# Half-chunk score loads, other places for fills, sums and weight passes, and another order of the first FFN matmuls in a fused scan and feed-forward kernel

## The chip, the cores and the metric

One core of one Trainium2 chip runs the whole kernel. The metric is the device time of one execution in microseconds (us), as a median over runs. The engines are named as in the profile: PE is TensorE (matmuls, with PEld for its weight loads), DVE is VectorE, ACT is ScalarE, POOL is GpSimd, and SP is SyncE, which here only issues DMAs. Each engine works through its own list in order; semaphores tie the lists together.

## The reference

Two parts follow each other. The first is a chunked linear-attention scan over 4 batches, 8 heads and 768 tokens, with head size 32 and state size 16; the second is a feed-forward network (FFN) on the 3072 tokens by 256 channels that come out of it. Cut to what matters:

```python
log_a = np.log(np.clip(a, 1e-06, 1.0))
for c in range(nc):                                   # chunks of tokens
    cum = np.cumsum(la, axis=-1)
    L = np.exp(cum[..., :, None] - cum[..., None, :]) * causal
    CB = np.einsum('bhin,bhjn->bhij', Cc, Bc)
    y_intra = np.einsum('bhij,bhjd->bhid', CB * L, xc)
    y_inter = np.einsum('bhin,bhnd->bhid', Cc, state) * np.exp(cum)[..., None]
    y[:, :, sl] = y_intra + y_inter
    state = decay_full * state + np.sum(Bx * decay_from_j, axis=2)

h = x @ w_in                                          # 256 -> 2048
g = np.maximum(0.01 * h, h)
out = g @ w_out                                       # 2048 -> 256
```

All of it is in float32.

## The kernel before, in words

The scan is cut into **units**: one chunk of 96 tokens of one batch, with its 8 heads. There are 8 chunks of 4 batches, so 32 units, and unit `u` is batch `u % 4` of chunk `u // 4`. A unit needs four things in turn. `decay_direct` (units 0 and 1) or `decay_pe` (units 2 to 15) makes the exponent of the decay mask on PE, and `decay_of` takes its exponential on ACT into the tile `lt`. `scores` multiplies B and C on PE, in two halves, and DVE multiplies each half onto `lt` (L314). `unit_products` multiplies the result with x and makes the next state (L326, L335). `unit_halves` copies the output, rounded to a high part `xh`, on ACT, puts the state into the next chunk's tile by way of POOL (L360), and subtracts on DVE to get the low part `xl` (L365). Units 16 to 31 take another way to their decay mask and are done in pairs between FFN steps (`pair_block`).

**The lead** is everything up to the first FFN step: the constants, the sums of the log decays, and units 0 to 14. Its loop stands at L619. In round `u` it issues the scores of unit `u + 1`, the decay mask of unit `u + 2` and the products of unit `u`. `fill_later` and `fill_less` write constant rows into the operands `dl` and `dr` of `decay_pe`, of which there are two sets, for 2 and for 4 units (`ROWS`); other rows of them come by DMA from the sums, which `split_sums` cuts into three bf16 parts and writes to DRAM (L605) and `decay_rows_of` reads back (L242, L245). Set 0 is used by units 2 and 3, set 1 by units 4 to 7. `keep_warm` issues a dummy matmul that nothing reads (L110). `score_tile` hands out one of two PSUM buffers of two banks each; a unit's scores use both.

**The FFN** works in 96 steps, each one tile of 512 tokens (`t`) with one block of 128 hidden columns (`f`); the first 21 steps go through `f` = 0 to 6 for three token tiles in turn, so steps 0, 1, 2 share `f` = 0. A step has two halves that stand apart: `ffn_in` (6 matmuls at L512 into a PSUM tile `hp`), and, three steps later (`LAG`), `ffn_out` (6 matmuls at L540). Between them ACT writes the activation's high part `gh` (L519) and the activation itself in place (L522), and DVE subtracts the two to get the low part `gl` (L525). Every float32 product is made of three: high times high, low weight times high, high weight times low. `hp` comes from `ps_h`, which has two buffers; steps 2 and 3 take a score tile instead.

**The weights** of a block `f` arrive as 64-bit floats in `raw` (512 KB, `fetch_w`) and are decoded by ACT and DVE: `decode_abs` on ACT, then five DVE *passes* in the order hold (L416), shift (L422), sign (L429), low (L436), rest (L449), with ACT's `decode_high` (L442) before rest. `rest` writes the low half `wl`. The passes stand in one queue; `LEAD_PASSES` says in which rounds of the lead one pass each is taken from it, and `PASSES` how many are taken after each FFN step. At step 0 two more are taken ahead of unit 15.

**The order** of all this is the order in which the code is written: the scheduler is switched off (`manual_schedule`), so each engine gets its instructions, and SP its DMAs, in the order of the calls.

## Time and profile before

| | us |
|---|---|
| Timed runs | 325.27, 325.07, 323.19 (median 325.07) |
| The profiled execution: own time / span in the profile | 323.83 / 322.1 |
| PE busy / its share of the span | 315.7 / 98% |
| DVE, ACT, POOL busy | 163.7, 167.4, 75.5 |
| First FFN matmul starts at | 36.72 |
| Its first `ffn_out` matmul starts at | 42.26 |

Times in the profile count from the start of the span. A row of the timeline reads: start, duration, engine, line, operation, output and inputs, shapes, count, and in brackets the idle time ahead of it and what ended it. Matmuls are pipelined, so a row of several matmuls is longer than the distance to the next, and distances of starts are the safer measure. A row of the chain of waits reads: start, length, what the time went to.

### The profile page before, as it was taken

To read this page: it belongs to the slowest core of one execution; us is meant where nothing else is said; L and a number is where in the kernel's file an instruction comes from. 1 tells how busy PE (TensorE), PEld (TensorE's weight loads), DVE (VectorE), ACT (ScalarE), POOL (GpSimd) and SP (SyncE) were. 2 spreads that over 40 slices of the span, in tenths; PEclk is the share of its full clock that TensorE was granted. 3 is DMA by queue.
4 is the path that set the end of the run, shared out by engine and by line. 5 is a ranking of instruction groups with operands and counts; after the bars stand their busy time and mean duration, and the time that the engine had idled before them with its cause. 6 is when DMAs were issued, how large, how long until landed. Compare 5 with 4: busy or idle time off the path is not lost.

```text
span 322.1 us, 6238 instructions
## 1 busy us (share of the span) xinstructions
PE 315.7 (98%) x2425; PEld 250.4 (78%) x2425; DVE 163.7 (51%) x312; ACT 167.4 (52%) x335; POOL 75.5 (23%) x162
## 2 busy tenths in 40 slices
PE   8999999999999999999999999999999999999995
PEld 4566688888887877788778788888878788888884
DVE  6878899888889325425352352524352322322221
ACT  5567686666576555454634636363633444444431
POOL 4377610000000163264330434344210000000000
PEclk9999999999999999999999999999999999999999
DMA  5687244323540830408120062202010000100001
GB/s 177 191 256 242 67 132 130 130 85 113 196 155 14 250 79 7 146 2 240 68 87 0 36 207 67 87 2 86 2 65 0 2 0 2 65 1 0 2 1 65
DMA packets 11497, 27.86 MB, mean 87 GB/s; under 512 B 2283, under 2 KB 2763, under 8 KB 11467
## 3 DMA queue, kind: packets, MB, share of 16 engines
q1 hardware_dynamic: 11323, 27.33, 27.4%
q8 instruction: 19, 0.31, 0.4%
q10 hardware_dynamic: 144, 0.13, 0.1%
q14 instruction: 11, 0.09, 0.1%
HBM read 24.14 MB, written 3.32 MB: 85 GB/s over the span
## 4 chain that ended last, share of the span: by engine, by line
PE 92%; DVE 3%; ACT 2%; issue 1%; ACTq 0%
PE hp L512 39%; PE py L540 35%; PE sc L540 5%; PE sc L386 2%; PE sc L326 2%; PE sc L309 2%; DVE lt L314 1%; PE pd L252 1%; PE py L326 1%; PE sc L512 1%; PE sc L110 1%; ACT lt L265 1%; PE py L226 1%; DVE dr L178 1%; PE sc L198 0%
## 5 line engine op out<-in xcount | busy, mean ns | idle before, releaser
L525 DVE TENSOR_TENSOR gl<-hp,gh 128x512 fp32r<-128x512 f32 x94 | 65.0, 691 | 140.6 <-ACT hp L522 140.6
L519 ACT ACTIVATE gh<-hp 128x512 fp32r<-128x512 f32 x94 | 56.1, 597 | 109.8 <-PE hp L512 109.8
L512 PE MATMUL hp<-xh,wl 128*128 128x512 f32 x188 | 73.3, 390 | 0.1
L512 PE MATMUL hp<-xh,wh 128*128 128x512 f32 x188 | 73.4, 390 | 0.0
L512 PE MATMUL hp<-xl,wh 128*128 128x512 f32 x188 | 73.2, 389 | 0.0
L540 PE MATMUL py<-gh,wh 128*128 128x512 f32 x164 | 65.3, 398 | 0.0
L540 PE MATMUL py<-gh,wl 128*128 128x512 f32 x164 | 63.9, 390 | 0.0
L540 PE MATMUL py<-gl,wh 128*128 128x512 f32 x164 | 63.9, 389 | 0.0
L522 ACT ACTIVATE hp<-hp 128x512 f32<-128x512 f32 x94 | 55.7, 593 | 0.0
L512 PEld LDWEIGHTS hp<-xh,wl 128*128 128x128 f32 x188 | 35.3, 188 | 7.8 <-DVE wl L449 0.5
L512 PEld LDWEIGHTS hp<-xl,wh 128*128 128x128 f32 x188 | 35.3, 188 | 7.3
L512 PEld LDWEIGHTS hp<-xh,wh 128*128 128x128 f32 x188 | 35.3, 188 | 7.3
L275 POOL TENSOR_TENSOR lt<-lt,ccol 112x768 f32<-112x768 f32 x16 | 23.5, 1469 | 67.1 <-DMA lt<-crow_d 66.6
L360 POOL COPY xs<-stage 16x64 f32<-16x64 f32 x112 | 27.7, 247 | 44.3 <-ACT stage L357 28.6
L540 PEld LDWEIGHTS py<-gh,wh 128*128 128x128 f32 x164 | 30.8, 188 | 9.0 <-issue 2.0
L540 PEld LDWEIGHTS py<-gl,wh 128*128 128x128 f32 x164 | 30.8, 188 | 6.5
L540 PEld LDWEIGHTS py<-gh,wl 128*128 128x128 f32 x164 | 30.8, 188 | 6.0
L284 POOL TENSOR_SCALAR_AFFINE_SELECT lt<-lt 96x768 f32<-96x768 f32 x16 | 14.0, 875 | 42.8 <-ACT lt L283 42.8
L314 DVE TENSOR_TENSOR lt<-sc,lt 112x384 f32<-112x384 f32 x32 | 16.3, 552 | 4.6 <-PE sc L309 2.0
L265 ACT ACTIVATE lt<-pd 112x768 f32<-112x768 f32 x15 | 12.1, 810 | 9.0 <-PE pd L252 5.8
L283 ACT ACTIVATE lt<-lt 112x768 f32<-112x768 f32 x16 | 13.5, 841 | 5.3 <-POOL lt L275 5.3
L395 DVE TENSOR_TENSOR lt<-sc,lt 112x384 f32<-112x384 f32 x32 | 15.6, 550 | 0.5
(101 smaller groups left out, 290.5 us busy)
## 6 DMA issues: line engine op xcount, KB each, us to landing
raw<-w_l SPq DMA_DIRECT2D x16, 512.0 KB, 4.7
lt<-crow_d SPq DMA_DIRECT2D x16, 336.0 KB, 5.5
bc<-bc_l SPq DMA_DIRECT2D x8, 608.0 KB
xs<-x_l SPq DMA_DIRECT2D x16, 192.0 KB, 5.4
out_l<-ob SPq DMA_DIRECT2D x11, 256.0 KB, 2.1
bn<-bn_l SPq DMA_DIRECT2D x8, 231.0 KB, 4.9
out_l<-obh ACTq DMA_DIRECT2D x1, 128.0 KB
out_l<-obh SPq DMA_DIRECT2D x1, 128.0 KB
```

Source lines behind the costliest of these rows:

```text
L265: nc.scalar.activation(heads, space[:QE, :, :4 * Q], AF.Exp)
L275: nc.gpsimd.tensor_tensor(out=lts[u], in0=lts[u], in1=ccol[:, u * NH:(u + 1) * NH].unsqueeze(2).to_broadcast([QE, NH, Q]), op=ALU.subtract,)
L283: nc.scalar.activation(lt, lt, AF.Exp)
L284: nc.gpsimd.affine_select(out=lt[:Q], in_=lt[:Q], pattern=[[0, NH], [1, Q]], compare_op=ALU.is_ge, fill=0.0, base=0, channel_multiplier=-1,)
L314: nc.vector.tensor_tensor(out=heads, in0=sc[:QE, :, :2 * Q], in1=heads, op=ALU.mult)
L360: nc.gpsimd.tensor_copy(to[:, :, hh], stage[hh * D:hh * D + N])
L395: nc.vector.tensor_tensor(out=heads, in0=spaces[half][:QE, :, 2 * Q * e:2 * Q * (e + 1)], in1=heads, op=ALU.mult,)
L512: nc.tensor.matmul(hp, lhsT=w_half[half][:, f, k * 128:(k + 1) * 128], rhs=x[t][:, k, :], start=(n == 0), stop=(n == 5),)
L519: nc.scalar.activation(ghs[s], hp, AF.Prelu, alpha=0.01)
L522: nc.scalar.activation(hps[s], hps[s], AF.Prelu, alpha=0.01)
L525: nc.vector.tensor_tensor(out=gls[s], in0=hps.pop(s), in1=ghs[s], op=ALU.subtract)
L540: nc.tensor.matmul(op, lhsT=w_half[half][:, f, DM + m * 128:DM + (m + 1) * 128], rhs=x, start=(first and i == 0), stop=(last and i == 2),)
```

## The change

The inputs of the scores (`bc`, 608 KB for a chunk) are laid out and loaded by half chunks of two batches, 304 KB each, in four buffers instead of two whole ones; the loads of the first chunk go out as half scores, half x, `bn`, half scores, half x, and those of chunks 2 and 3 one round or more earlier for the first half. The constant rows are filled at other places: the `dl` part (`fill_sources`) of set 0 ahead of the clamp of `la` and of set 1 ahead of unit 0's scores; the `dr` part of set 1 behind unit 0's scores; of the four `fill_less` of set 1 two go to POOL and two on DVE behind unit 1's scores. The sums stand between the two units' mask matmuls. Of the dummies the one ahead of the column sums and the one ahead of unit 1's scores go; the one ahead of unit 2's stays.

The weight passes of the lead are five instead of seven, in rounds 7, 8, 9, 11, 13 instead of 9, 10, 11, 12, 13, 14, 14, and `decode_abs(0)` goes from round 7 to round 6.

In `ffn_in` the four matmuls with the high weights come ahead of the two with the low ones. Step 3 takes an `hp` tile instead of a score tile, and `ffn_out(1)` moves from behind `ffn_in(4)` to ahead of `ffn_in(3)`.

```diff
-B_COLS = NB * QE
-C_COLS = NB * 2 * Q
+B_COLS = NB // 2 * QE
+C_COLS = NB // 2 * 2 * Q
...
-LEAD_PASSES = (9, 10, 11, 12, 13, 14, 14)
+LEAD_PASSES = (7, 8, 9, 11, 13)
...
-    pbc = ctx.enter_context(tc.tile_pool(name="pbc", bufs=2))
+    pbc = ctx.enter_context(tc.tile_pool(name="pbc", bufs=4))
+    pbn = ctx.enter_context(tc.tile_pool(name="pbn", bufs=2))
...
-    def fetch_bc(c, eng=nc.sync):
-        bcs[c] = pbc.tile([128, BC_COLS], F32, name="bc")
-        eng.dma_start(bcs[c], bc_l[c])
+    def fetch_bc(c, g):
+        bcs[c, g] = pbc.tile([128, BC_COLS], F32, name="bc")
+        nc.sync.dma_start(bcs[c, g], bc_l[c, g])
...
-    fetch_bc(0)
+    fetch_bc(0, 0)
     for c in range(3):
         alloc_x(c)
-    fetch_x(0)
+    fetch_x(0, (0,))
     fetch_bn(0)
+    fetch_bc(0, 1)
+    fetch_x(0, (1,))
...
-    def fill_later(i):
+    def fill_sources(i):
         n = ROWS[i]
         nc.vector.memset(dls[i][Q:], 1.0)
         nc.vector.memset(dls[i][Q:Q + 3 * NH, :, Q:], 0.0)
         nc.vector.tensor_copy(dls[i][:Q], upto_b.unsqueeze(1).to_broadcast([Q, n, QE]))
+
+    def fill_later(i):
+        n = ROWS[i]
         nc.vector.tensor_copy(
...
-        if s in (2, 3):
+        if s == 2:
             hp = score_tile()[:, 0]
...
-        for k in range(2):
-            for half, x in ((0, xh), (1, xh), (0, xl)):
+        for halves in (((0, xh), (0, xl)), ((1, xh),)):
+            for k, (half, x) in ((k, h) for k in range(2) for h in halves):
...
+        fill_sources(0)
         nc.vector.tensor_scalar(
...
-        for u in range(DIRECT):
-            decay_mask(pds[u])
+        decay_mask(pds[0])
         split_sums(first[:, 0, :Q])
+        decay_mask(pds[1])
...
-        second = score_tile()
-        keep_warm(second[:, 1], WARM2)
-        columns(erev, after, AF.Exp, second[:, 0])
-        fill_later(1)
+        columns(erev, after, AF.Exp, score_tile()[:, 0])
         nc.sync.dma_start(parts_d, parts)
         decay_direct(0, pds[0])
         decay_of(0, pds[0])
+        fill_sources(1)
         decay_rows_of(DIRECT)
+        fetch_bc(1, 0)
         decay_rows_of(DIRECT + ROWS[0])
-        fetch_bc(1)
         fetch_bn(1)
-        fetch_x(1)
+        fetch_x(1, (0,))
+        fetch_bc(1, 1)
+        fetch_x(1, (1,))
+        for b in range(2, ROWS[1]):
+            fill_less(1, b, nc.gpsimd.tensor_copy)
         scores(0)
+        fill_later(1)
         state_decay(0)
-        for b in range(ROWS[1]):
-            fill_less(1, b, nc.vector.tensor_copy)
         decay_direct(1, pds[1])
         decay_of(1, pds[1])
         for u in range(PE_DECAY - 1):
-            scores(u + 1, 1 if u < 2 else 0)
+            scores(u + 1, 1 if u == 1 else 0)
+            if u == 0:
+                for b in range(2):
+                    fill_less(1, b, nc.vector.tensor_copy)
...
+            if u in (1, 2, 5, 6):
+                fetch_bc((u + 7) // 4, u % 4 - 1)
             if u in (2, 6):
-                fetch_bc(u // 4 + 2)
                 state_decay((u + 2) // 4)
...
-            if u == 7:
+            if u == 6:
                 decode_abs(0)
             decode(LEAD_PASSES.count(u))
...
         if s == LAG:
 
             ffn_out(0)
+            ffn_out(1)
...
-        if s > LAG:
+        if s > LAG + 1:
             ffn_out(s - LAG)
```

Three places show what moves. The first is DVE around the scores of units 0, 1 and 2. `dl` and `dr` are the operands with the constant rows, `later` and `less` the constants, `sc` a half of the scores, `lt` the decay mask. Before:

```order
L170 COPY dl4_120<-upto_b_115 96x448
L171 COPY dr4_122<-later_117 96x3072
L314 TENSOR_TENSOR lt_186<-sc_199,lt_186 112x384
L314 TENSOR_TENSOR lt_186<-sc_203,lt_186 112x384
L178 COPY dr4_122<-less_118 24x768 x4
L314 TENSOR_TENSOR lt_214<-sc_216,lt_214 112x384
L314 TENSOR_TENSOR lt_214<-sc_221,lt_214 112x384
L314 TENSOR_TENSOR lt_254<-sc_256,lt_254 112x384
```

And in the changed kernel:

```order
L173 COPY dl4_125<-upto_b_120 96x448
L321 TENSOR_TENSOR lt_186<-sc_206,lt_186 112x384
L321 TENSOR_TENSOR lt_186<-sc_210,lt_186 112x384
L177 COPY dr4_127<-later_122 96x3072
L321 TENSOR_TENSOR lt_218<-sc_220,lt_218 112x384
L321 TENSOR_TENSOR lt_218<-sc_224,lt_218 112x384
L184 COPY dr4_127<-less_123 24x768 x2
L321 TENSOR_TENSOR lt_259<-sc_261,lt_259 112x384
```

The four copies of `less` between units 0 and 1 have become the one copy of `later`, and two copies of `less` stand between units 1 and 2; the other two are on POOL.

The second is PE from the end of `ffn_in(4)` to the start of `ffn_in(5)`; `hp` and `sc` are the steps' PSUM tiles. Before:

```order
L512 MATMUL hp_947<-xh_450,wl_145 128x512
L512 MATMUL hp_947<-xl_451,wh_144 128x512
L540 MATMUL sc_965<-gh_895,wh_144 128x512
L540 MATMUL sc_965<-gh_895,wl_145 128x512
L540 MATMUL sc_965<-gl_896,wh_144 128x512
L540 MATMUL sc_965<-gh_895,wh_144 128x512
L540 MATMUL sc_965<-gh_895,wl_145 128x512
L540 MATMUL sc_965<-gl_896,wh_144 128x512
L512 MATMUL hp_972<-xh_662,wh_144 128x512
```

And in the changed kernel, from `ffn_in(3)` (`hp_941`) on:

```order
L520 MATMUL hp_941<-xl_248,wh_149 128x512
L520 MATMUL hp_941<-xh_247,wl_150 128x512 x2
L520 MATMUL hp_959<-xh_457,wh_149 128x512
L520 MATMUL hp_959<-xl_458,wh_149 128x512
L520 MATMUL hp_959<-xh_457,wh_149 128x512
L520 MATMUL hp_959<-xl_458,wh_149 128x512
L520 MATMUL hp_959<-xh_457,wl_150 128x512 x2
L520 MATMUL hp_978<-xh_673,wh_149 128x512
```

The six matmuls of `ffn_out(1)` no longer stand between `ffn_in(4)` and `ffn_in(5)`; steps 3, 4 and 5 follow each other, and `hp_978` takes the buffer of `hp_941`.

The third is DVE behind the low part of unit 6 (`py_480`, later `py_489`). Before:

```order
L365 TENSOR_TENSOR xl_451<-py_480,xh_450 128x2x96
L314 TENSOR_TENSOR lt_520<-sc_553,lt_520 112x384
L314 TENSOR_TENSOR lt_520<-sc_557,lt_520 112x384
L365 TENSOR_TENSOR xl_451<-py_522,xh_450 128x2x96
L314 TENSOR_TENSOR lt_564<-sc_593,lt_564 112x384
```

And in the changed kernel:

```order
L372 TENSOR_TENSOR xl_458<-py_489,xh_457 128x2x96
L424 TENSOR_SCALAR w32_518<-w32_518 128x512
L321 TENSOR_TENSOR lt_531<-sc_563,lt_531 112x384
L321 TENSOR_TENSOR lt_531<-sc_567,lt_531 112x384
L372 TENSOR_TENSOR xl_458<-py_533,xh_457 128x2x96
L430 TENSOR_SCALAR w32_518<-w32_518 128x512
L321 TENSOR_TENSOR lt_574<-sc_604,lt_574 112x384
```

The hold (L424) and shift (L430) passes of the first weights now stand ahead of the score products of units 9 and 10; before, they stood two rounds later.

## The prediction

> **What bounds the kernel now.** I read the chain that ended last first, then the stages, then the lead (everything ahead of the first FFN matmul at 36.72) row by row. The page's chain, by engine:

> ```profile
> PE 92%; DVE 3%; ACT 2%; issue 1%; ACTq 0%
> ```

> The stages (length, then busy time of PE, PEld, DVE, ACT, POOL, then clock, DMA share, GB/s):

> ```profile
> 14.12:24.15 10.03, 10.03 (x262) 6.64 (x253) 7.79 (x21) 6.87 (x20) 6.72 (x26) 1.00 0.85 247
> 24.15:36.72 12.57, 12.08 (x302) 7.89 (x293) 10.50 (x25) 9.25 (x25) 9.12 (x30) 1.00 0.55 179
> 42.26:59.00 16.74, 16.74 (x75) 13.89 (x74) 15.41 (x29) 12.11 (x23) 0.00 (x0) 1.00 0.43 134
> 59.00:250.00 191.00, 190.60 (x1315) 154.99 (x1315) 95.71 (x171) 100.72 (x197) 51.48 (x83) 1.00 0.29 89
> ```

> From 42.26 to 250 PE is idle for 0.4 us, and the change takes no matmul from it there. What the change can win lies before 42.26. There, two stretches lose time. The starts of three units' scores on PE (units 3, 9 and 15):

> ```profile
> 14.12 0.63 PE L309 MATMUL sc<-bc 32*112 32x192 f32 x8
> ...
> 24.15 0.63 PE L309 MATMUL sc<-bc 32*112 32x192 f32 x8
> ...
> 35.38 0.82 PE L309 MATMUL sc<-bc 32*112 32x192 f32 x8
> ```

> Units 3 to 9 take 10.03 us, 1.67 each, with PE busy all the time. Units 9 to 15 do the same work in 11.23: 1.20 us are lost where the weight passes stand. The other stretch, in the chain of waits:

> ```profile
> 8.90 0.55 DVE lt L314
> ...
> 9.48 1.11 DVE dr L178 x3
> ...
> 11.48 0.57 DVE lt L314
> ...
> 12.10 0.38 PE sc L110
> ```

> Between the score products of units 0 and 1 DVE makes four constant fills, and PE waits for it until 12.10.

> **The early part.** Rows of the first units:

> ```profile
> 4.59 0.63 PE L110 MATMUL sc<-idle 128*128 128x512 bf16 x1
> ...
> 5.01 1.06 PE L198 MATMUL sc<-la,after 96*112 96x256 f32 x2
> ...
> 5.87 1.92 PE L226 MATMUL py<-reach,after 96*112 96x384 f32 x4
> ...
> 6.98 0.95 DVE L171 COPY dr<-later 96x3072 bf16<-96x3072 bf16 x1
> ...
> 8.24 1.54 PE L226 MATMUL pd<-reach,after 96*112 96x384 f32 x4
> ...
> 9.48 1.97 DVE L178 COPY dr<-less 24x768 bf16<-24x768 bf16 x4
> ...
> 9.82 0.81 ACT L265 ACTIVATE lt<-pd 112x768 f32<-112x768 f32 x1 [1.51 <-PE pd L226]
> ```

> The dummy ahead of the column sums holds PE from 4.59 to 5.01, 0.42 us. The same four matmuls take 1.92 at 5.87 and 1.54 at 8.24, so PE is still at a lower pace at first, and work that moves forward runs at that pace: the dummy is worth between 0.2 and 0.42, and I take 0.25. That puts unit 1's exponential at 9.57 and its end at 10.38. On DVE unit 0's products end at 9.20 instead of 9.45; the one copy of `later` (0.95) follows and ends at 10.15, hidden with 0.25 to spare. So unit 1's products can start at about 10.5 instead of 11.48, and unit 2's dummy and scores move by the same 1.0. Two fills (half of 1.97) then stand ahead of unit 2's products, which start at 12.4 instead of 13.10; unit 3's second half waits for its score buffer by about 0.1. At unit 3 the gain is 0.9. Its ends are 0.25 (only the dummy, something else holds unit 1 or 2) and 1.0. If the cover of the `later` copy goes, it costs what exceeds 0.25.

> Two fills go to POOL, where the trace has no copy of that shape; its nearest rows are the two selects of 96x768 and the page's subtraction of 112x768:

> ```profile
> 3.61 2.07 POOL L181 TENSOR_SCALAR_AFFINE_SELECT reach<-la 96x768 f32<-96x768 f32 x2 [0.89 <-ACT la L591]
> ...
> 7.97 1.06 POOL L290 TENSOR_TENSOR bn<-bn,erev 112x512 f32<-112x512 f32 x1 [2.28 <-DMA bn<-bn_l]
> ...
> 10.81 0.31 PE L335 MATMUL py<-xs,bn 96*32 96x32 f32 x16
> ```

> ```profile
> L275 POOL TENSOR_TENSOR lt<-lt,ccol 112x768 f32<-112x768 f32 x16 | 23.5, 1469 | 67.1 <-DMA lt<-crow_d 66.6
> ```

> At 1.0 to 1.5 each they end at 7.7 to 8.6, since POOL is free at 5.68, and the state product (1.06) behind them at 8.8 to 9.7. Its reader, L335, comes at about 10.2. Cost nothing; without that cover, up to the overrun. `bn` itself, for which POOL waited 2.28 us, is now third in the queue, with 496 KB less ahead of it.

> The `dl` fills of set 0 go into DVE's wait for `la`, those of set 1 into its wait for unit 0's scores: nothing. The sums move ahead of two mask matmuls, so the DRAM round trip of their parts starts earlier, ahead of what needs it. The halves of `bc` add eight DMA issues on SP, each no dearer than the 0.42 of the weight load shown below, in a queue that mostly waits; the list of PE's waits in the lead names no DMA. One of them now stands between the row loads of set 0 and set 1; set 1 is first read by unit 4, whose mask comes two units behind unit 2's.

> **The passes.** The rows around the loss:

> ```profile
> 24.05 1.06 POOL L290 TENSOR_TENSOR bn<-bn,erev 112x512 f32<-112x512 f32 x1
> 24.06 0.35 DVE L365 TENSOR_TENSOR xl<-py,xh 128x192 fp32r<-128x192 f32 x1
> ...
> 31.22 1.05 POOL L290 TENSOR_TENSOR bn<-bn,erev 112x512 f32<-112x512 f32 x1
> ...
> 31.45 1.37 DVE L429 SCALAR_TENSOR_TENSOR w<-raw,w 128x512 uint32<-128x512 uint32 x1
> ...
> 33.35 1.04 PE L309 MATMUL sc<-bc 32*112 32x192 f32 x8 [0.45 <-DVE lt L314]
> ```

> ```profile
> 39.48 0.68 DVE L429 SCALAR_TENSOR_TENSOR w<-raw,w 128x512 uint32<-128x512 uint32 x1
> ```

> The sign pass took 1.37 beside POOL's state product and 0.68 without it, and PE then waited 0.45. I read that as DVE held back by POOL, for 0.69. In the changed kernel sign, in round 9, is clear of a state product, but hold, in round 7, comes right behind the L365 that starts with the product of 24.05, and low, in round 11, stands where sign stood. Two such meetings cost PE 2 x 0.45 = 0.9; between them there is one pass a round, and 1.67 a round leaves DVE room for that. [...]

> `decode_abs(0)` moves one round ahead on ACT, behind the row at 22.75, and its data may not be there:

> ```profile
> 18.01 0.42 SPq L82 DMA_DIRECT2D raw<-w_l  x1
> ...
> 22.75 0.33 ACT L362 CAST xh<-py 128x192 fp32r<-128x192 f32 x1
> ...
> 23.66 0.81 ACT L265 ACTIVATE lt<-pd 112x768 f32<-112x768 f32 x1 [0.58 <-PE pd L252]
> ```

> ```profile
> DMA to landing us min/median/max: 6.0/6.0/6.0
> ```

> ```profile
> raw<-w_l SPq DMA_DIRECT2D x16, 512.0 KB, 4.7
> ```

> Those weights landed at 24.0. With the lead 0.95 ahead, ACT is ready at 22.1, and the load goes out at 17.05: landing after 4.7, as is usual, is 21.75, no wait; after 6.0 it is 23.05, a wait of 0.95. Behind it in ACT's queue stands unit 9's exponential, for which unit 10's mask matmul (one buffer) and unit 9's products wait; PE has some 0.25 of room. That is 0 to 0.7 for PE, in the same place as the meeting of hold (0.45), which it covers or exceeds; I take 0.5 for both. The passes then lose 0.5 + 0.45 = 0.95 of the former 1.20: gain 0.25, ends 1.20 and -0.9 (the load as late as before, worked out below).

> **The first steps.** PE rows of step 0, and of the end of step 3 with the starts of the two blocks behind it:

> ```profile
> 36.72 0.50 PE L512 MATMUL hp<-xh,wh 128*128 128x512 f32 x1
> 37.35 0.50 PE L512 MATMUL hp<-xh,wl 128*128 128x512 f32 x1
> ...
> 44.76 0.39 PE L512 MATMUL sc<-xl,wh 128*128 128x512 f32 x1
> 44.99 0.39 PE L512 MATMUL hp<-xh,wh 128*128 128x512 f32 x1
> ...
> 46.35 0.39 PE L540 MATMUL sc<-gh,wh 128*128 128x512 f32 x1
> ```

> Matmuls start 0.23 apart (44.76 to 44.99), in step 0 0.63: a wait of 0.40 for the low weights. Now low and ACT's copy come a round earlier, and the low weights are read as fifth and sixth: this 0.40 goes. What is late next is nothing in steps 0 to 4: `ffn_out(1)`, now ahead, reads a `gl` that DVE writes behind no more than one sign and one low pass, with a whole `ffn_out` on PE ahead of it. But steps 3, 4 and 5 now follow each other on two `hp` buffers. What reads step 3's buffer last:

> ```profile
> 46.31 0.69 DVE L525 TENSOR_TENSOR gl<-sc,gh 128x512 fp32r<-128x512 f32 x1
> ```

> Step 3's successor starts at 44.99 and the block behind that at 46.35, which now would be step 5; the buffer is free at 46.31 + 0.69 = 47.00. A new wait of 47.05 - 46.35 = 0.70, with everything on PE behind it. It costs 0.70 (0.6 to 1.0, if DVE, 92% busy from 42.26 on, has a pass in the way). The rest of the FFN keeps its matmuls and its order but for the high halves first, whose `xl` is made long before: nothing.

> **The sum.** 0.9 + 0.25 + 0.40 - 0.70 = 0.85 us off. The profiled execution took 323.83 (span 322.1 and 1.7 around it) and would take 323.0. It lies 1.24 below the median of the runs shown, 325.07, and 0.64 above the lowest; the four of them average 324.34. I set the sum against that average: 323.5.

> **The rivals.** *The lead loses nothing any more* (the passes meet no state product, the weights are there): 0.9 + 1.20 + 0.40 - 0.70 = 1.8, so 322.5. For it: sign, the longest, is clear, and one pass a round fits. Against it: the places of hold and low beside rows 24.05 and 31.22.

> *The weights land no earlier than before*, at 24.0, since the DMA engines are the limit (0.85 busy from 14.12 to 24.15, and the same bytes go ahead of them). ACT then waits 1.9, PE 1.65, with low 2.1 against the former 1.20: 0.9 - 0.9 + 0.40 - 0.70 = -0.3, slower, 324.6. It turns slower once the landing is later than about 23.7. Against it: the loads of chunk 1, the first of those bytes, go out behind sums that are made earlier, and only as far as the queue is never empty does an earlier start count in full. [...]

> *The early gain is only the dummy's*, because the row loads or POOL's fills hold unit 2: 0.25 + 0.25 + 0.40 - 0.70 = 0.2, so 324.1. Against it: the covers above.

> **Chances.** Forecast 0.48, lead without loss 0.27, weights late 0.12, early gain lost 0.13. One per cent, about what a measurement of this kernel can tell from no change, is 3.2 us: no case reaches it, the best that all terms could give without the new wait is 0.9 + 1.2 + 0.4 = 2.5. Only the scatter between runs (2.1 from lowest to highest) can carry a case across: faster by over 1% 0.07, slower 0.04, within 0.89. The range goes from the best rival less that scatter's lower half, 322.5 - 1.1 = 321.4, to the worst with its upper, 324.6 + 0.9 = 325.5.

> **What would show it.** Right: unit 1's first L314 product near 10.5, unit 3's scores near 13.1, hold (L416 before) over 0.9 long, low over 1.2, no gap of 0.4 between the first two matmuls of step 0, and a gap near 0.7 ahead of step 5 that ends on DVE's `gl`. Wrong: ACT waiting for `raw` ahead of its first decode (second rival), passes of usual length and 1.67 a unit up to unit 15 (first), unit 1 or 2 waiting for row loads or POOL (third), or no gap at step 5.

## The result, and the profile after

The changed kernel takes 326.60 us (median of 22 executions, 324.18 to 331.87); the kernel before, between them on the same chip, 324.26 (22 executions, 323.19 to 325.27). The ratio is 1.0071, with a 95% interval of 1.0050 to 1.0091: slower by 0.7%, within the 1% that the forecast called no change, but 3.1 above its 323.5 and outside its range of 321.4 to 325.5. The ratio, here and below, leaves out executions more than 1.5% above the fastest of a kernel; the medians leave out none.

The profiled execution took 326.58, 2.75 more than the 323.83 before (span 324.8 against 322.1). The starts on PE:

| start of | before | after | after less before |
|---|---|---|---|
| unit 3's scores | 14.12 | 12.97 | -1.15 |
| unit 9's scores | 24.15 | 24.91 | +0.76 |
| unit 15's scores | 35.38 | 37.62 | +2.24 |
| step 0 | 36.72 | 38.73 | +2.01 |
| from step 0 to the end of the span | 285.41 | 286.11 | +0.70 |

So the early part gained more than forecast, the rest of the lead lost 3.16, and the steps lost 0.70. The chain that ended last, by engine, and what PE waited for (total us, times, longest):

```profile
PE 92%; DVE 2%; issue 2%; ACT 1%; DMA 1%; SPq 0%; ACTq 0%
```

```profile
PE py L333 <- issue: 2.4, 3, 1.0
...
PE pd L258 <- ACT lt L271: 0.8, 2, 0.7
PE pd L258 <- DMA dl<-parts_d: 0.8, 1, 0.8
PE sc L204 <- DVE ob L577: 0.8, 1, 0.8
PE hp L520 <- DVE gl L533: 0.5, 1, 0.5
```

The DVE fills that stood in the chain before (DVE 3%) have left it. The largest wait is new: 2.4 us in three pieces for "issue", that is, for nothing that the profile shows. PE's timeline has them, each inside a row of equal products (L333) that wait for nothing:

```profile
17.34 0.53 PE L333 MATMUL py<-lt,xs 112*32 112x96 f32 x12
18.36 0.36 PE L333 MATMUL py<-lt,xs 112*32 112x96 f32 x4 [0.50 <-issue]
...
23.10 0.52 PE L333 MATMUL py<-lt,xs 112*32 112x96 f32 x11
24.49 0.28 PE L333 MATMUL py<-lt,xs 112*32 112x96 f32 x3 [0.87 <-issue]
...
29.92 0.52 PE L333 MATMUL py<-lt,xs 112*32 112x96 f32 x11
31.43 0.28 PE L333 MATMUL py<-lt,xs 112*32 112x96 f32 x3 [1.00 <-issue]
```

Counted from 0 at PE's first record, with matmuls, weight loads, semaphore and drain instructions together, the records behind the three gaps are numbers 449, 705 and 961: 256 apart. The page has a queue for instructions, q8, beside that of the loads (packets, MB, share of 16 engines):

```profile
q1 hardware_dynamic: 12475, 27.33, 28.0%
q8 instruction: 19, 0.31, 0.4%
```

In the trace's DMA records those 19 packets have 16384 bytes each. PE has 4911 records in all, and 19 x 256 is 4864: that fits one packet for 256 of them, 64 bytes each. In the lead one of them goes in each block of 256 instructions that PE works through. The three that end ahead of the gaps (here and below, a gap at one of these records is the distance of its start from the start of the record ahead of it; 0.06 is no wait):

| PE enters a block of 256 at | fetch of the next block | PE enters the next at | gap there | same in the kernel before: entry, fetch, next entry, gap |
|---|---|---|---|---|
| 12.59 | 15.63 to 16.88 | 18.36 | 0.75 | 13.72, 15.41 to 16.52, 18.68, 0.06 |
| 18.36 | 21.77 to 22.89 | 24.49 | 1.12 | 18.68, 21.07 to 22.11, 23.75, 0.06 |
| 24.49 | 28.88 to 29.98 | 31.43 | 1.25 | 23.75, 26.14 to 27.06, 29.08, 0.06 |

PE goes on 1.45 to 1.61 us behind the end of the fetch. Three units at 1.67 are 256 instructions, 5.0 us. With 1.1 for the fetch and some 1.4 behind it, 2.5 us are left between PE's entry into a block and the start of the next fetch; before, the two longest were 2.39, with which PE lost nothing, and after they are 3.0, 3.4 and 4.4. By this estimate the kernel before stood some 0.1 us from these gaps. It is a rough one: its record 705 came 1.64 behind a fetch's end, and where PE stood waiting, in any of the profiles, it went on 1.20 to 1.72 behind. No view of waits says so.

Units 3 to 15 take 24.65 us here and would take 20.04 at 1.67 each; before, they took 21.26. Of the 4.6 us lost, the three gaps are 2.9 (each less 0.06), PE's wait for the exponential behind the late decode (L271 above) 0.7, and its wait for the products behind the low pass 0.3.

The other row that is new is ACT's wait for the weights, with DVE's first pass (hold) and its fourth (low):

```profile
24.75 0.67 ACT L419 ACTIVATE w<-raw 128x512 f32<-128x512 f32 x1 [1.98 <-DMA raw<-w_l]
```

```profile
25.45 0.43 DVE L424 TENSOR_SCALAR w<-w 128x512 f32<-128x512 f32 x1 [1.35 <-ACT w L419]
...
33.82 1.25 DVE L444 SCALAR_TENSOR_TENSOR w<-raw,w 128x512 uint32<-128x512 uint32 x1
```

And the first steps: the second matmul of step 0 follows 0.34 behind the first (0.63 before), and step 5 starts at 49.91, where 48.75 + 2 x 0.23 = 49.21 would be without the wait:

```profile
38.73 0.50 PE L520 MATMUL hp<-xh,wh 128*128 128x512 f32 x1
39.07 0.40 PE L520 MATMUL hp<-xl,wh 128*128 128x512 f32 x1
...
48.75 0.61 PE L520 MATMUL hp<-xh,wl 128*128 128x512 f32 x2
49.91 0.50 PE L520 MATMUL hp<-xh,wh 128*128 128x512 f32 x1 [0.55 <-DVE gl L533]
```

### The profile page after: what moved, and what is told of

Read it like the earlier page. It is cut to its first block, busy times and chain, and to the rows that moved or that the text cites. A ratio compares the mean times of both kernels' runs of the same rounds, so it can differ in the third digit from the quotient of the medians.

```text
span 324.8 us, 6245 instructions
## 1 busy us (share of the span) xinstructions
PE 314.3 (97%) x2423; PEld 249.2 (77%) x2423; DVE 163.0 (50%) x310; ACT 167.5 (52%) x335; POOL 77.1 (24%) x164
## 4 chain that ended last, share of the span: by engine, by line
PE 92%; DVE 2%; issue 2%; ACT 1%; DMA 1%; SPq 0%; ACTq 0%
PE hp L520 39%; PE py L548 35%; PE sc L548 5%; PE sc L394 2%; PE py L333 2%; PE sc L333 2%; PE sc L316 2%; PE pd L258 2%; DMA parts_d<-parts 1%; PE py L342 1%; PE sc L111 1%; DMA dl<-parts_d 1%; ACT lt L271 0%; DVE lt L321 0%; PE sc L342 0%
## 5 line engine op out<-in xcount | busy, mean ns | idle before, releaser
L533 DVE TENSOR_TENSOR gl<-hp,gh 128x512 fp32r<-128x512 f32 x95 | 65.7, 691 | 140.1 <-ACT hp L530 140.0
L527 ACT ACTIVATE gh<-hp 128x512 fp32r<-128x512 f32 x95 | 56.8, 598 | 109.9 <-PE hp L520 109.9
L520 PE MATMUL hp<-xh,wh 128*128 128x512 f32 x190 | 74.3, 391 | 0.5 <-DVE gl L533 0.5
L520 PE MATMUL hp<-xh,wl 128*128 128x512 f32 x190 | 58.5, 389 | 0.0
L290 POOL TENSOR_SCALAR_AFFINE_SELECT lt<-lt 96x768 f32<-96x768 f32 x16 | 14.0, 875 | 41.3 <-ACT lt L289 41.3
L271 ACT ACTIVATE lt<-pd 112x768 f32<-112x768 f32 x15 | 12.2, 811 | 8.2 <-PE pd L258 5.5
## 6 DMA issues: line engine op xcount, KB each, us to landing
raw<-w_l SPq DMA_DIRECT2D x16, 512.0 KB, 3.4
```

Of the source, the lines that this page charges most:

```text
L290: nc.gpsimd.affine_select(out=lt[:Q], in_=lt[:Q], pattern=[[0, NH], [1, Q]], compare_op=ALU.is_ge, fill=0.0, base=0, channel_multiplier=-1,)
L520: nc.tensor.matmul(hp, lhsT=w_half[half][:, f, k * 128:(k + 1) * 128], rhs=x[t][:, k, :], start=(n == 0), stop=(n == 5),)
L527: nc.scalar.activation(ghs[s], hp, AF.Prelu, alpha=0.01)
L533: nc.vector.tensor_tensor(out=gls[s], in0=hps.pop(s), in1=ghs[s], op=ALU.subtract)
```

## The experiments

The first theory, T: PE's instruction fetches stand in line with the loads of the lead, and the half loads make them later. Rivals: R1, being ahead is enough, whatever is loaded; R2, the loss is the late weights. Eighteen kernels ran, in five groups, each with runs of the kernel before on the same chip; medians of different groups are compared by their distance from it. Of each kernel 12 executions were timed; the first of them is the profiled one.

### First group: halves, loads, steps

**e1_whole**, the changed kernel with whole loads again:

```diff
-        fetch_bc(1, 0)
         decay_rows_of(DIRECT + ROWS[0])
+        fetch_bc(1)
         fetch_bn(1)
-        fetch_x(1, (0,))
-        fetch_bc(1, 1)
-        fetch_x(1, (1,))
+        fetch_x(1)
...
-            if u in (1, 2, 5, 6):
-                fetch_bc((u + 7) // 4, u % 4 - 1)
             if u in (2, 6):
+                fetch_bc(u // 4 + 2)
```

> The changed kernel with the score columns of a chunk loaded whole again, at the places where the kernel before issues them; everything else (fills, sums, dummy, passes, high halves first, two hp buffers) as changed. Theory T (TensorE's own instruction fetches, on queue q8, run behind the loads of the lead; halves brought earlier and in rows of 2432 B make them later): the three gaps of 0.75, 1.12 and 1.25 us in the middle of L333 products shrink to at most one of them under 0.5, ScalarE's wait for raw falls from 2.0 to under 1.0, step 0 starts near 36.7 - 1.1 = 35.6 to 36.3 instead of 38.73, and the time is 326.6 - 2.5 = 324.1, with 323.5 to 324.8 as its range. Rival R1 (the fetch of 256 instructions takes 4.3 to 4.9 us in the kernel before already, against blocks of 5.0 us; TensorE being 1.15 us ahead eats this, whatever is loaded): gaps of together 1 us or more stay, step 0 at 37.5 or later, 325.5 to 326.6. Rival R2 (the loss is the late weights alone): gaps stay or not, the wait for raw stays near 2.0 and the time at 326.

Measured: 327.86 (323.57 to 333.23), ratio 1.0026 (0.9984 to 1.0068). The profiled execution took 332.9 and showed what no theory had: PE at about half its usual pace for 30 us. Its rows, with the four matmuls of 384 columns that were L226 in the kernel before (2.77 us), and two rows of a unit's scores:

```profile
5.62 2.77 PE L230 MATMUL py<-reach,after 96*112 96x384 f32 x4
...
29.06 0.99 PE L314 MATMUL sc<-bc 32*112 32x192 f32 x8
...
32.80 0.59 PE L314 MATMUL sc<-bc 32*112 32x192 f32 x8
```

The same four products in the changed kernel's profile, and then a window of 2 us of each, e1_whole first (length, busy time of PE, PEld, DVE, ACT, POOL with counts, granted clock, DMA share, GB/s):

```profile
5.17 1.45 PE L232 MATMUL py<-reach,after 96*112 96x384 f32 x4
```

```profile
26.00:28.00 2.00, 2.00 (x30) 0.96 (x22) 0.60 (x2) 0.69 (x3) 0.93 (x4) 1.00 0.49 195
```

```profile
20.00:22.00 2.00, 2.00 (x74) 1.44 (x63) 1.71 (x6) 1.44 (x5) 1.21 (x6) 1.00 1.05 284
```

Both windows call PE busy all the time at a granted clock of 1.00. For the first this is no reading: in e1_whole's trace the first record of the clock, at full speed, begins at 29.9 us, and the view counts time without a record as full. The counts, 30 and 74, and the lengths of equal rows tell the pace. At that pace PE needs 2.76 us a unit and shows no gap (one fetch started 0.4 us ahead of PE's entry, the next 1.5 behind): T, R1 and R2 stayed untested here.

**e2_halves**, the kernel before with the half loads alone:

```diff
-        fetch_bc(1)
+        fetch_bc(1, 0)
...
+            if u in (1, 2, 5, 6):
+                fetch_bc((u + 7) // 4, u % 4 - 1)
             if u in (2, 6):
-                fetch_bc(u // 4 + 2)
```

> The kernel before with nothing changed but the loads of the score columns: halves, four buffers, at the places of the changed kernel. Theory T (loads delay the instruction fetches): gaps of 0.3 to 1.2 us appear in TensorE's row of products at every 256th instruction of the lead, put down to issue, 1 to 2.5 us in sum, ScalarE waits for raw over 0.5, and the time is 325.3 to 326.8 against 324.3 before. Rival R1 (being ahead alone): no gap over 0.2, since TensorE is no earlier than before; time within 0.4 of before. Rival R2 (late weights alone): no gaps in the products, but a wait for raw of 1 to 2 us at the first decode, and a time up to 1 us above before.

Measured: 324.65 (323.83 to 326.23), 1.0010 (0.9984 to 1.0036). In the profile PE's gaps at the 449th, 705th and 961st instruction are 0.06, 0.18 and 0.44, the fetches start 2.86 and 3.27 behind PE's entry (2.39 before), and step 0 starts 0.59 later. T has the direction, at a quarter of its size; the time lies below T's 325.3 to 326.8, and nothing can be told from it.

**e3_noload**, the changed kernel without the score loads of chunks 1 to 3:

```diff
     def fetch_bc(c, g):
+        if 0 < c < 4:
+            bcs[c, g] = bcs[0, g]
+            return
```

> The changed kernel without the loads of the score columns of chunks 1 to 3: their scores are taken with chunk 0's B and C, so the outputs that follow from these chunks are others. Six half loads of 311 KB each, 1.87 MB, are gone from the lead; TensorE's instructions stay the same. Theory T: no gap over 0.2 at the 256th instructions, fetches start within 1.5 us of TensorE's entry into the block ahead and land 1 us later, no wait for raw, step 0 starts before 35.8, time 323.0 to 324.0. Rival R1 (being ahead alone, no loads needed): gaps of together over 1 us stay, since the fetch takes as long with an empty queue; step 0 not before 37. Rival R2 (late weights): raw lands early, so 324.5, with the gaps in the products as they were.

Measured: 323.27 (322.95 to 333.41), 0.9960 (0.9933 to 0.9987). Nine of 12 executions lie between 322.95 and 324.43, as T has it, with step 5's wait still in them. The profile (333.41) was one at the lower pace, without gaps.

**e4_steps**, the changed kernel with steps 2 to 5 as before:

```diff
-        if s == 2:
+        if s in (2, 3):
             hp = score_tile()[:, 0]
...
-            ffn_out(1)
...
-        if s > LAG + 1:
+        if s > LAG:
```

> The changed kernel with steps 2 to 5 as they were before: step 3's hidden products in the score tile, the output products of step 1 at their old place. The lead is as changed. Theory T and all rivals but one: the wait of TensorE for VectorE's gl ahead of step 5 (row idle 0.50, start of the step 0.70 late) goes, and the time is 326.6 - 0.7 = 325.9 (325.5 to 326.3); the gaps in the lead stay. The rival to it (that the wait only takes the place of one that comes later, at the late sums): time within 0.2 of the changed kernel, 326.4 to 326.8.

Measured: 327.38 (323.57 to 332.04), 1.0059 (1.0020 to 1.0098): no lower than the changed kernel, against the 325.9 expected. The profile (329.14) has PE at the lower pace until 17 us and one gap of 1.79 at the 961st instruction. But from step 0 to the end it has 285.24 where the changed kernel has 286.11: the wait at step 5 is gone, and the time is hidden under a lead that varies by more.

### Second group: the dummy

The four dummies that PE starts with had not changed; but the one ahead of the column sums was gone. The theory that the pace hangs on it, W, was tried from both sides.

**f1_dummy** puts it back, **f2_whole_dummy** with whole loads as well, **f3_nodummy** takes it from the kernel before:

```diff
+        second = score_tile()
+        keep_warm(second[:, 1], 1)
-        columns(erev, after, AF.Exp, score_tile()[:, 0])
+        columns(erev, after, AF.Exp, second[:, 0])
```

> The changed kernel with one thing put back: the dummy matmul ahead of the column sums (at 4.59 in the profile before). Theory W (without it TensorE stays at its lower pace, four L232 products in 2.77 instead of 1.45 us, until 17 to 30 us in part of the executions, and these are the ones of 327 to 333 us): full pace by 7 us, no execution over 328.4, highest less lowest below 4 us; the gaps at every 256th instruction and the wait for raw stay as far as the half loads cause them, so the median is 325.3 (324.3 to 326.3). Rival D (the dummy is worth its 0.25 to 0.42 us and no more): the executions spread as those of the changed kernel, 324 to 332, with a median of 326.9.

> The changed kernel with the dummy put back and the score columns loaded whole again at their old places. Theories W and T (half loads delay TensorE's instruction fetches and raw) together: full pace by 7 us, no gap over 0.3 in the products of the lead, a wait for raw under 1.0, step 0 at 35.6 to 36.4, all executions within 2.5 us of each other, median 323.7 (323.1 to 324.4). Rival R1 (being ahead is enough to run out of instructions): gaps of together 0.8 us or more in the lead, step 0 at 36.7 or later, 324.6 to 325.8. Rival D: executions up to 333 again.

```diff
-WARM2 = 1
+WARM2 = 0
```

> The kernel before without its dummy ahead of the column sums, and nothing else. Theory W: the executions fall apart, some near 323.8 and 2 to 6 of 12 between 326.5 and 333; where the profile is one of those, four L226 products at 5.5 take 2.8 instead of 1.92 us and the units 2.76 us each instead of 1.67. Rival D (the dummy only costs time): all executions between 322.9 and 325.3, median 0.1 to 0.4 below before. Rival P (the other places of the fills and sums, not the dummy, make TensorE too idle to reach its pace): as D, no execution over 327.2.

Measured: f1_dummy 326.19 (324.76 to 333.32), 1.0061 (1.0026 to 1.0096); f2_whole_dummy 325.36 (324.51 to 330.31), 1.0050 (1.0012 to 1.0088); f3_nodummy 327.47 (323.31 to 332.98), 1.0046 (1.0001 to 1.0090). Without its dummy the kernel before falls apart as W says, 5 executions up to 324.56 and 7 from 327.35 on. But W's "no execution over 328.4" failed in the other two: f1_dummy has two over it (328.72 and 333.32) and f2_whole_dummy three. One dummy is not enough where the sums stand ahead of the second mask product.

For T against R1 the profile of f2_whole_dummy speaks against T: with whole loads the gaps are still 0.57 and 1.13, and step 0 is at 37.34. And f3_nodummy shows R1 on the kernel before itself. Its PE ran 0.62 ahead at unit 8 (21.80 against 22.42). It entered its block at 18.07 instead of 18.68, the fetch began at 21.38, not earlier than the 21.07 before, and a gap of 0.53 at the 705th instruction ate the lead exactly, so that unit 9 starts at 24.16 (24.15 before) and step 0 at 36.71 (36.72):

```profile
23.74 0.28 PE L326 MATMUL py<-lt,xs 112*32 112x96 f32 x3 [0.29 <-issue]
...
24.16 0.59 PE L309 MATMUL sc<-bc 32*112 32x192 f32 x8
...
36.71 0.50 PE L512 MATMUL hp<-xh,wh 128*128 128x512 f32 x1
```

**f4_best** was meant to keep the gains: dummy, whole loads, old steps 2 to 5, and

```diff
-            if u == 6:
+            if u == 7:
                 decode_abs(0)
...
-LEAD_PASSES = (7, 8, 9, 11, 13)
+LEAD_PASSES = (9, 10, 11, 12, 13)
```

> A version meant to take what is left of the gains: the changed kernel with the dummy put back, whole loads, steps 2 to 5 as before, the first decode a round later (round 7) and the five passes in rounds 9 to 13. By W and T: early part 0.9 minus the dummy's 0.25, step 0's wait for the low weights gone (0.40), no wait at step 5, lead losses between 0.6 and 1.2 as before: 324.3 - 0.65 - 0.4 = 323.2 (322.3 to 323.8), with all executions within 2.5 us. If being ahead runs TensorE out of instructions (R1), the 0.65 is eaten: 323.9 or more.

Measured: 323.64 (322.95 to 328.10), 0.9990 (0.9957 to 1.0024). No wait for `raw`, none at step 5; the gaps at the 705th and 961st instruction are 0.48 and 0.82, and step 0 starts at 36.68, so 1.67 of lead at unit 3 (12.45 against 14.12) came to 0.04. R1's way, at the time that W and T gave; but two executions, 327.78 and 328.10, lie outside the 2.5 us that they gave for all.

### Third group: bytes

In the profiles at full pace the DMA engines do next to nothing between 7.5 and 9.5 us (a share of 0.17, 0.00, 0.00 and 0.04 in the half us of the changed kernel's profile, 0.01, 0.00, 0.00 and 0.17 before), while SP waits for the sums' round trip, and are then busy, mostly 0.8 to 1.1, to 30. Theory B joins T and R1: fetches wait behind the bytes that were asked for ahead of them.

**g1_best_hole** and **g2_after_hole** move two loads of chunk 1 into the hole, in f4_best and in the changed kernel:

```diff
         nc.sync.dma_start(parts_d, parts)
+        fetch_bn(1)
+        fetch_x(1, (0,))
```

> The version f4_best, with two loads of chunk 1 (its B rows and the first half of x, 423 KB) issued right behind the store of the split sums instead of behind the row loads, so that they go while the DMA engines have nothing (7 to 9.5 us in every profile so far). Theory B (the lead is bound by bytes: the DMA engines are 0.85 to 1.06 busy from 10 to 30 us, and TensorE's instruction fetches stand in line with the loads, so that whoever is early waits for them): 423 KB at some 270 GB/s is 1.6 us earlier for all that follows; fetches start 1 to 1.6 us earlier, the gaps of 0.48 and 0.82 at the 705th and 961st instruction go, step 0 starts at 35.2 to 35.9 instead of 36.68, and the time is 323.6 - 1.1 = 322.5 (322.0 to 323.1). Rival R1 (a fetch takes its 4.5 to 5 us whatever else is loaded): gaps as before, 323.4 to 324.0. Against both: the row loads, now behind these bytes, may hold unit 2 by up to 1 us.

> The changed kernel with the same two loads of chunk 1 put into the same hole and nothing else. Theory B: gaps at the 449th, 705th and 961st instruction of together 3.1 us fall to under 1.6, the wait for raw from 2.0 to under 1.0, step 0 from 38.73 to 37.2 or earlier; time 326.6 - 1.5 = 325.1 (324.3 to 325.8). Rival R1: unchanged, 326.2 to 327.

Measured: g1_best_hole 323.82 (322.88 to 331.88), 0.9983 (0.9963 to 1.0004), no better than f4_best. Its profile has step 0 at 36.24, 0.44 earlier, gaps of 0.53 and 0.36, and a new wait of 0.50 for POOL's state product, which now waits for its own load:

```profile
8.41 1.86 POOL L294 TENSOR_TENSOR bn<-bn,erev 112x512 f32<-112x512 f32 x1 [1.43 <-DMA bn<-bn_l]
```

By 21 us it had moved 4403 KB, f4_best 4490: the later loads went out no earlier (`raw` at 16.99, in f4_best at 16.60), so the bytes pulled forward were not followed by others, and B's 1.6 us did not come. g2_after_hole 329.61 (323.32 to 333.88), 1.0051 (1.0004 to 1.0099): ten of 12 executions above 327, its profile (329.83) at the lower pace until 16 us. Nothing on B can be read from it; with this order executions above 328 were more frequent still, 8 of 12.

**g3_extra** gives the kernel before 608 KB more to move:

```diff
                 fetch_bc(u // 4 + 2)
+                if u == 2:
+                    nc.sync.dma_start(extra_d, bc_l[3])
```

> The kernel before with 608 KB more to move in the lead: behind the load of chunk 2's score columns (15.2 us) a copy of as many bytes within DRAM, which nobody reads. Theory B: from there on all is 2.2 us later in the queue; TensorE, which had no gap over 0.06 at its 256th instructions, gets gaps there of together 1 to 3 us, raw is waited for, step 0 starts 1 to 3 us after 36.72, time 325.3 to 327.3. Rival R1, and any by which only the lead's own order counts: no gaps, within 0.4 of before.

Measured: 325.27 (324.56 to 329.72), 1.0026 (0.9997 to 1.0055), the median 0.9 above before: more than the 0.4 that R1 allowed, and at the lower end of B's range. The profile shows the path. A gap of 0.81 at the 705th instruction, whose fetch started 3.40 behind PE's entry, a wait for x and one for the weights, and step 0 at 38.79, 2.07 later. Some 1.3 of this, an estimate from the starts of the units, is PE's lower pace, which came back behind these waits (below):

```profile
PE pd L253 <- DMA xs<-x_l: 0.9, 1, 0.9
PE py L327 <- issue: 0.6, 1, 0.6
```

```profile
ACT w L412 <- DMA raw<-w_l: 0.5, 1, 0.5
```

**g4_noload_dummy** is e3_noload with the dummy.

> The changed kernel with the dummy put back and without the loads of the score columns of chunks 1 to 3 (the scores of these chunks are taken with chunk 0's B and C, so their outputs are others); 1.82 MB are gone from the lead, TensorE's instructions are those of f1_dummy. Theory B: no gap over 0.2, no wait for raw, fetches start within 1.5 us of TensorE's entry into a block, step 0 at 34.6 to 35.6, time 322.8 to 323.6 with step 5's wait still in it. Rival R1: gaps of together 1 us or more as in f1_dummy (2.0) stay, step 0 at 37 or later, 324.5 or more.

Measured: 323.86 (323.29 to 334.42), 0.9977 (0.9957 to 0.9996); ten of 12 executions between 323.29 and 324.77, where f1_dummy, with the loads, has eight between 324.76 and 326.40. Between the medians of these two clusters, 323.7 and 325.1, lie 1.4 us for 1.8 MB less. That is B's sign from the other side; the profile (334.42, lower pace until 33 us) shows no gaps, but neither do e1_whole's and e3_noload's at that pace.

### Fourth group: three dummies

**h1_after3**, **h2_best3** and **h3_before3** are the changed kernel, f4_best and the kernel before with three dummies at that place. Against f1_dummy and f4_best, one line changes; in the kernel before it is `WARM2` that becomes 3:

```diff
-        keep_warm(second[:, 1], 1)
+        keep_warm(second[:, 1], 3)
```

> The changed kernel with three dummies ahead of the column sums instead of none. Theory W+B (the low pace comes by chance where TensorE's first microseconds are not dense enough; the rest of the loss is late instructions and late raw): at most 1 of 12 executions over 328, full pace by 7 us in the profile, gaps at the 256th instructions and a wait for raw together still over 1.5 us, median 325.6 (324.8 to 326.4): the low pace then carries about 1 us of the 2.3 lost, the gaps the rest. Rival: the low pace does not depend on the dummies; 3 or more of 12 over 328, median 326.5 or more.

> The version f4_best with three dummies ahead of the column sums instead of one. W+B: no execution over 326, median 323.9 (323.4 to 324.5): two dummies cost 0.4 to 0.8 us early, of which the gaps at the 705th and 961st instruction give back a part. Rival (dummies do nothing for the pace): 2 of 12 near 328 as before, median 324.2.

> The kernel before with three dummies there instead of one. Price of two dummies: at most 0.86, by the 0.42 between the starts of the one dummy and of the sums behind it; W: highest less lowest under 2 us (the kernel before has 10 of 92 executions over 326.4), median 324.6 (324.1 to 325.2). Rival: median 324.1 and the same scatter.

Measured: h1_after3 325.16 (324.19 to 327.37), 1.0043 (1.0018 to 1.0068); h2_best3 323.60 (322.87 to 324.84), 0.9991 (0.9969 to 1.0013); h3_before3 324.69 (323.71 to 327.78), 1.0032 (1.0007 to 1.0057), beside 323.76 for the kernel before in this group. No execution of the 36 is over 328, and the three profiles are at full pace by 6.6: W holds for the start. The narrow spread that it gave h3_before3, under 2 us, did not come (4.07). The changed kernel lay 2.34 above the kernel before beside it, h1_after3 lies 1.40 above: three dummies bring 0.9 although they cost time (0.9 in the kernel before). What is left is late instructions (gaps of 1.39 and 1.66, wait for raw 1.6, step 0 at 39.34, in a profile of 327.19, with PE at the lower pace again behind the second gap) and step 5. In h2_best3's profile the fetches came in time, PE has one gap of 0.21, and step 0 starts 1.14 earlier than before, with an execution of 322.87:

```profile
35.58 0.50 PE L518 MATMUL hp<-xh,wh 128*128 128x512 f32 x1
35.91 0.39 PE L518 MATMUL hp<-xl,wh 128*128 128x512 f32 x1
```

**h5_late** is the kernel before with the late half of the change alone:

```diff
-LEAD_PASSES = (9, 10, 11, 12, 13, 14, 14)
+LEAD_PASSES = (9, 10, 11, 12, 13)
...
-        for k in range(2):
-            for half, x in ((0, xh), (1, xh), (0, xl)):
+        for halves in (((0, xh), (0, xl)), ((1, xh),)):
+            for k, (half, x) in ((k, h) for k in range(2) for h in halves):
```

> The kernel before with the late half of the change alone: high halves first in the FFN's hidden products, five passes in rounds 9 to 13 ahead of the first step instead of seven in 9 to 14. Step 0's wait of 0.40 goes; the early part, the loads and the lead's order up to round 14 are as before: 324.2 - 0.4 = 323.8 (323.3 to 324.2). If f4_best stays below it by 0.2 or more, the early half is worth that; if they are equal, the early half is worth nothing once TensorE's instructions set the lead (B).

Measured: 324.21 (323.38 to 326.09), 1.0010 (0.9988 to 1.0032), not the 323.8 expected. Step 0's wait is gone (37.39 to 37.73), but from step 0 to the end the profile has 285.58, against 285.41 before. The wait at the late sums, 0.4 before, became 0.7:

```profile
PE sc L198 <- DVE ob L569: 0.7, 1, 0.7
```

```profile
PE sc L198 <- DVE ob L569: 0.4, 1, 0.4
```

(h5_late first, then before.) The 0.40 is real and is not kept. h2_best3, in the same group, lies 0.6 below h5_late, and f4_best, in another, as far; by h5_late's expectation that is what the early half is worth. The intervals overlap, so it is not shown.

### Fifth group: steps and decode, with the pace held

Both start from h1_after3. **i1_steps** undoes steps 2 to 5, with e4_steps' diff; **i2_later** the earlier decode, with f4_best's.

> The changed kernel with three dummies, and steps 2 to 5 as before (step 3's hidden products in the score tile again). If the wait at step 5 (start 0.70 late) is paid in full: 325.16 - 0.7 = 324.5 (324.1 to 324.8), no row of TensorE waiting for gl. If something behind it takes its place: 325.0 or more.

> The changed kernel with three dummies, the first decode back in round 7 and the passes in rounds 9 to 13; half loads and step 5 as changed. If the wait for raw (1.6 us on ScalarE in h1_after3) costs TensorE what the profiles show (0.2 to 0.7): 324.6 (324.3 to 325.0), wait for raw under 0.8. If TensorE's late instructions hide it (they are later anyway): within 0.2 of h1_after3, 325.0 to 325.4, with the gaps as there.

Measured: i1_steps 324.08 (322.98 to 328.21), 1.0004 (0.9980 to 1.0029): 1.08 less than h1_after3 (1.47 less by the distances from the kernel before), more than the 0.7 expected. In the profile PE waits for no `gl`, and from step 0 to the end there are 285.22 instead of 286.13, so 0.91 of it is read there. i2_later 325.72 (324.20 to 328.30), 1.0050 (1.0028 to 1.0071): no gain. Its profile has neither gaps nor a wait for `raw`, and step 0 at 36.10; but at 324.32 it is the second fastest of the 12 executions and does not stand for the others. What the first decode a round earlier costs in the time stays open.

### The two readings over all profiles

*Instructions.* In the 20 profiles, PE's records 449, 705 and 961 stand behind 22 gaps of 0.2 us or more, in 15 of the profiles; all 22 end 1.20 to 1.72 us behind the end of a fetch. The five without are the kernel before, i2_later, and three at the lower pace. The order of the lead puts all 22 into the same row of products (`py<-lt,xs`, L326 before), at a matmul or a weight load. The same row of the units between has no such gap in any profile: it goes by the count of instructions, not by the line.

*Pace.* Every profiled execution of 329 us and more (five) shows PE at the lower pace from the start until 16 to 34 us; every one up to 327.2 (fifteen) is at full pace by 8.1. The traces' records of the granted clock agree: the first one, at full speed, begins at 15.9 to 34.0 in the five and at 4.5 to 7.4 in the fifteen.

They show a second thing. In f1_dummy, g2_after_hole, g3_extra, h1_after3 and i1_steps the clock falls to 0.50 later in the lead, for 3.4 us, at most 1.6 us after PE had waited 1.3 to 1.8 us (in g3_extra in two pieces). The rows follow it. In f1_dummy, where the record says 25.7 to 29.1, the scores of a unit are long once, and two units take 4.66 us instead of 3.34:

```profile
24.71 0.28 PE L333 MATMUL py<-lt,xs 112*32 112x96 f32 x3 [1.76 <-issue]
...
25.13 0.59 PE L316 MATMUL sc<-bc 32*112 32x192 f32 x8
...
27.49 1.00 PE L316 MATMUL sc<-bc 32*112 32x192 f32 x8
...
29.79 0.59 PE L316 MATMUL sc<-bc 32*112 32x192 f32 x8
```

So a gap can cost more than its own length. Not every one does: behind e4_steps' gap of 1.79 the clock stays. One such fall takes 0.005 off the mean clock that each execution lists (3.4 us at 0.50 in a span of some 324; the profiled executions of f1_dummy, h1_after3 and i1_steps list 0.995). By that mark (0.995 or less) 9 of 22 executions of the changed kernel had one, though not the profiled one; of the kernel before, in the five groups, 15 of 165; of e3_noload, g4_noload_dummy, f4_best and h2_best3 none of 48. Executions above 328, by what stands ahead of the column sums:

| kernels | dummies there | executions above 328 | of these without such a fall |
|---|---|---|---|
| after, e1, e3, e4, g2, and f3 (order before) | none | 31 of 82 | 23 |
| f1, f2, f4, g1, g4 (sums ahead of the second mask) | one | 12 of 60 | 7 |
| before in its six groups of runs, e2, g3, h5 (order before) | one | 5 of 223 | 0 |
| h1, h2, i1, i2, and h3 (order before) | three | 2 of 60 | 0 |

The last column leaves out the executions in which such a fall can be the reason. What is left fits the lower pace from the start, and W shows more clearly there: 23, 7, 0 and 0.

## Why the prediction was wrong

**What bounds the kernel.** That little changes behind the lead but step 5 held: from step 0 to the end all profiles lie between 285.22 and 286.50. The lead was read as PE's and DVE's; that it was also, by the estimate above, within a few tenths of a us of being the instruction fetch's is the part that was missed.

**The early part.** The mechanism was right, and at unit 3 its gain was 1.15 instead of 0.9, above its upper end of 1.0. Unit 1's first product started at 9.51, not 10.5, since PE was at full pace sooner than in the profile before (the four products 1.45 long instead of 1.92). The `later` copy stayed hidden, and POOL's state product ended at 8.32, ahead of the 8.8 to 9.7 worked out. One cover failed as the third rival had it: the store of the split sums was said to start earlier, and SP issued it at 6.41 instead of 6.07:

```profile
6.41 0.35 SPq L611 DMA_DIRECT2D parts_d<-parts  x1
```

```profile
6.07 0.35 SPq L605 DMA_DIRECT2D parts_d<-parts  x1
```

(after, then before), so that PE, now early, waited 0.79 for the rows at unit 2's mask.

**Two steps failed.** The first is that the gain at unit 3 was carried to the end of the sum. PE that is ahead enters each block of 256 instructions earlier, the fetch comes no earlier, and the gap takes the lead back; f3_nodummy's profile shows it with one edit, 0.62 in and 0.01 out. In the changed kernel the three gaps, 2.9 us, took more than the whole lead. That it is the bytes asked for ahead of a fetch that hold it is supported by e3_noload, g3_extra and g4_noload_dummy; it is not shown, since g1_best_hole, which moved bytes out of the way, gained nothing in the time. The halves add to it (e2_halves: the fetch behind the entry at the 705th instruction starts 3.27 us later, before 2.39), but whole loads alone do not cure it (f2_whole_dummy).

The second is **the dummy, priced at a gain of 0.25.** PE's lower pace was read off two rows (1.92 against 1.54) as a cost of early work; whether the dummy has a part in ending it was not asked. Without it 31 of 82 executions were above 328, f3_nodummy shows the same with nothing else changed (4 of 12), and three dummies bring the changed kernel from 2.34 to 1.40 above the kernel before.

**The passes.** Of the two meetings with POOL, low came (1.25 long from 33.82, beside POOL's state product of 33.46 to 34.52, where the other 15 low passes take 0.68 to 0.69; forecast over 1.2; PE then waited 0.33, forecast 0.45), hold did not (0.43 long at 25.45, POOL's product from 23.75 to 24.81), since it was late itself: the weights landed at about 24.7, later than the slower rival's 24.0. That rival, at 0.12 and 324.6, had the right mechanism, and on ACT more than its price (1.98 against 1.9), but on PE less: 0.66 ahead of unit 10's mask, where it had 1.65. And the weights were one of several things behind the same bytes, the instructions among them, and i2_later could not show that they carry the time.

**Step 0** was right in its place, 0.34 instead of 0.63 between the matmuls, and wrong in what is kept: PE then waited 0.8 instead of 0.4 at the late sums. i1_steps and e4_steps, which have this order and the early decode with old steps 2 to 5, end 285.22 and 285.24 behind step 0, so 0.18 of the 0.40 is left; h5_late, with later passes, keeps none.

**Step 5.** Its start is 0.70 late, as worked out (the rows cited give 47.00 - 46.35 = 0.65; the prediction took 47.05). Undoing it takes 0.89 off the steps (286.12 to 285.23, each the mean of two profiles), so the term was a little too small.

The sum of what the profile after shows: lead +2.01 instead of -1.15, and +0.70 behind it instead of +0.30, so 2.71 slower instead of 0.85 faster. The medians moved by 2.34; a single profile does not hold the scatter of the executions. The median before, 324.26, was where the average of 324.34 had put it.

**A version for both.** h2_best3 is 3.0 below the changed kernel (323.60 against 326.60; 2.5 by the distances from the kernel before) and its 12 executions are the narrowest of all that have the early part, 1.97. Against the kernel before the ratio is 0.9991 (0.9969 to 1.0013): no difference that can be told.

**Open.** What decides whether a fetch comes in time: h1_after3 and i2_later differ only in where the first decode and the passes stand, and in their profiles the fetch behind PE's entry at the 705th instruction started 4.1 and 2.4 us later; one profile each does not say whether the decode did it. And what sets PE's clock: in e1_whole PE was busy in the records all the while that the lower pace lasted, and of waits of like length some were followed by a fall of the clock and some not.

## What to carry to other kernels

In a stretch of many short matmuls beside heavy loads, look for gaps called "issue" that stand a fixed number of records apart (256 here), and compare the time PE needs for so many instructions (5.0 us for three units here) with the fetch's wait, length and what follows it (2.4, 1.1 and some 1.4): being ahead was worth nothing in f3_nodummy while the fetch came no earlier (0.62 at unit 8, 0.01 at step 0). Then look whether equal rows get longer behind such a gap (4.66 us instead of 3.34 for two units in f1_dummy). The dummy at this kernel's start was not priced by its length (0.42) but by what the executions did without it (4 of 12 above 328 in f3_nodummy, 5 of 223 with it in the order before); take such a dummy out alone, in a dozen executions, before counting it as a gain. An early gain belongs in the sum only after each later limit of the same stretch has been asked whether it moves along.

## What the runs showed of the hardware

**TensorE's lower pace can last, and it can come back.** Equal rows took 1.9 times as long (2.77 in e1_whole against 1.45 in the changed kernel) until 16 to 34 us in five of the 20 profiles, by the times in part of the executions of one and the same program (e1_whole: 323.57 to 333.23). The records of the granted clock begin, at full speed, where this ends, so a view that gives 1.00 ahead of the first record does not show it. In five profiles the clock fell back to 0.50 for 3.4 us. The stretches at full clock between are 13.7, 20.5, 27.3 and 290.1 to 320.9 us long in the 20 traces (314.0 in the kernel before, 320.9 in the changed one). With three dummies ahead of the column sums, 0.65 to 1.28 us together, full pace came by 6.6 in the five profiles, and 58 of 60 executions stayed at or under 328. What sets the moment of the switch was not shown: in e1_whole, with PE busy for 28.74 of the first 30 us, it came at 29.9.
